# A long-convolution and Mish-MLP kernel: its visits on another calendar

## The chip, the cores and the metric

The kernel runs on one core of one Trainium2 chip. The metric is the device time of one execution in microseconds (us), lower is better; the time given for a version is the median of its runs. TensorE is called PE, its weight loads PEld; VectorE is DVE, ScalarE is ACT, GpSimd is POOL, and SyncE is SP, which here only issues DMAs.

## The reference

Two branches share one input of 2048 positions by 448 channels, and their sum is returned:

```
xn = layernorm(q)                                  # over the 448 channels
A: kv = (short causal convolution of k, 4 taps) * v
   y  = causal convolution of kv with ssm_k, 2048 taps per channel, by FFT
   A  = xn * (y + kv * ssm_D)
B: B  = mish(xn @ w1 + b1) @ w2                    # 448 -> 1792 -> 448
out  = q + A + B
```

## The kernel before

**The MLP sets the beat.** The positions are cut into 8 chunks of 256, and the 1792 hidden features into 7 pairs of 128, which makes 56 pairs in all (`pairs`). Each pair takes two half steps (`mlp_slot`). In an even half step 2i, PE does the first product of pair i (`g1_mm`, L449, 22 matmuls; every operand is split into a rounded part and a remainder, XH/XL, w1h/w1l, so that one product becomes three). In the odd half step 2i+1, ACT applies Mish (L457) and rounds (ach, L72), DVE forms the remainder (acl, L73), and PE does the second product (`g2_mm`, L474 to L476, 12 matmuls) of the pair two before. In what follows g1 and g2 are these two products.

**Once per chunk** come other steps, always at the same half steps: the layernorm statistics and POOL's normalising; four transposes each at half steps 14c+11 and 14c+12 (`ln_T`, L409), with their split into XH (ACT, L421) and XL (DVE, L419). The transposes take their PSUM tile from the same two buffers as g1, so the g1 of 14c+12 waits until the XL of 14c+11 is done. At 14c+18 the evacuation qt (`g2_evac`, L481, DVE) frees the two PSUM tiles into which the next chunk's first g2 writes, at 14c+19, and SP stores the result (L486).

**The FFT branch is fitted in between by a calendar.** The lists in the diff below give the half step of each visit; `plan` holds what is issued ahead of the half step's own work, `plan2` what comes behind it. The branch has four stages:

- f1 visits (`f1_mm`, L123), eight for h, the long filter (`H_AT`), and eight for kv (`KV_AT`). Each is followed by a fold: ACT copies one PSUM tile (L129), DVE adds and subtracts (L130, L132), and three half steps later ACT's queue stores st into Dh or Dkv (L138). st has two buffers.
- kv's taps on DVE, in four parts u0 to u3 per group, spread over the distance d between two visits of kv: u0 is one product (L152), u1 and u3 two half products and a sum (L154, L156, L161), u2 a product and a sum (L152, L161), and u3 ends with the product by v (L164). k and v are loaded by SP some half steps ahead (L143, L147).
- octets (`OCT_AT`: first half step, distance): per octet a visit to transform h (L197, one ahead), one for kv (L197), products on DVE (L230), and the first inverse transform i1 (L242) four later; its result qe goes to E in DRAM. `H0_AT` is the first of these visits.
- last steps (`I2_AT`: half step to two chunks): E is loaded (L277, SP for one chunk and POOL for seven), DVE folds e (L282, L284) three half steps ahead, PE does i2 (L300), and the gate follows (L310 to L318).

Queues run in order: what stands ahead of an instruction on its engine must have started first, and SP issues its DMAs one after the other, each when its own waits are over. The weights come as well: w1 and w2 are loaded and split over the first 16 half steps (`w1_split`, `w2_split`; w2l is the remainder, L73).

Of the kernel before, what the change touches and what calls it, by code (L numbers as in the profile page):

```python
# [22 lines left out]

G2_LAG = 2
H_HEAD = 1
H_AT = {2: 4, 3: 8, 0: 12, 4: 16, 5: 20, 6: 26, 7: 32}
KV_AT = (24, 29, 34, 39, 44, 50, 55, 60)
H0_AT = 63
OCT_AT = (65, 3)
I2_AT = {98: (6, 7), 102: (0, 1), 106: (2, 3), 111: (4, 5)}  # L30
LATE = 2
WARM = 3
WARM_N = 448
# [3 lines left out]
def tile_kernel(ctx: ExitStack, tc, q, k, v, sk, hT, sD, w1, b1, w2, c_f1, c_g, c_gi, c_i2, out):  # L37
# [51 lines left out]
    def at(slot, fn, *args):  # L89
        plan.setdefault(int(slot), []).append((fn, args))  # L90
# [182 lines left out]
    def e_load(c):  # L273

        e = EE[c] = t3([128, 2, 2, D], "e3", 4)
        src = E[:, :, :, :, c].rearrange("h j k m b d -> (j k m) h (b d)")
        (nc.sync if c == I2_AT[min(I2_AT)][1] else nc.gpsimd).dma_start(e.rearrange("p h b d -> p h (b d)"), src)  # L277

# [242 lines left out]

    for g, t in H_AT.items():
        if g != 2:
# [8 lines left out]
    for g in range(-2, 0):  # L532
        at(12, k_load, g)
    for g, t in enumerate(KV_AT):
        d = t - (KV_AT[g - 1] if g else t - 6)
        at(t - d - (3 if g > 1 else 2), k_load, g)
# [15 lines left out]
    for o in range(NO):  # L552
        s, d = OCT_AT[0] + OCT_AT[1] * o, OCT_AT[1]
        h = s - 1 if o else H0_AT
        at(h - d if o else h - 2, o_load, AH, Dh, o, "ah")
# [10 lines left out]

    ts = sorted(I2_AT)
    for n, t in enumerate(ts):
        for m, c in enumerate(I2_AT[t]):
            at(ts[n - 2] + 1 if n > 1 else ts[0] - 4 + n, e_load, c)  # L570
# [119 lines left out]
```

## Time and profile before

| | |
|---|---|
| median of 3 runs | 381.12 us (379.84 to 381.22) |
| profiled execution | 380.68 us, of it 378.9 us from first to last instruction |
| PE busy | 365.5 us (96%) |
| DVE busy | 270.0 us (71%) |
| ACT busy | 165.9 us (44%) |
| POOL busy | 52.7 us (14%) |
| mean granted PE clock | 0.994 |

PE is busy in nearly every slice, so the time is PE's work plus what it waits. A row of the waits names who waited, for whom, the sum in us, how often, and the longest. A row of the timeline has start, length, engine, line, operation, and in brackets the idle time ahead of it with what ended it. Matmuls overlap, so the distance from one start to the next tells more than a length.

### The profile page before, as it was taken

Reading aid. Unit: us, or ns where it says so; the run is one execution under the profiler, and the core shown is the slowest. Engines: PE = TensorE matmul, PEld = TensorE weight load, DVE = VectorE, ACT = ScalarE, POOL = GpSimd, SP = SyncE. Lnnn points to the kernel's source line nnn. Section 1 sums busy time; section 2 is a strip of 40 time slices with the busy share of each in tenths; the row PEclk is TensorE's granted clock in tenths of the full one; section 3 lists DMA queues with packets and bytes.
Section 4 is the critical chain, followed back from the end, with each engine's and each line's share of the span. In section 5 each row is a group of like instructions: output and inputs, shape, how many; then the busy total and the mean of one; then the engine's idle time right before and its main releaser. Section 6 shows DMA issues by size and latency. Waiting matters only on the chain.

```text
span 378.9 us, 7964 instructions
## 1 busy us (share of the span) xinstructions
PE 365.5 (96%) x3382; PEld 295.2 (78%) x3382; DVE 270.0 (71%) x357; ACT 165.9 (44%) x277; POOL 52.7 (14%) x46
## 2 busy tenths in 40 slices
PE   5999999999999999999999999999999999999994
PEld 1788888968888989889877666666666879889883
DVE  2889858999999998997525747655465733897651
ACT  2677553343341443243353555545465433225440
POOL 2106100700033001400005000060000002112101
PEclk9899999999999999999999999999999999999999
DMA  7699996829587429514775498897495477739927
GB/s 269 246 293 354 363 337 159 251 80 284 134 283 220 98 62 271 162 43 99 242 240 201 138 273 233 264 269 212 144 289 159 91 195 300 258 150 317 185 68 145
DMA packets 31988, 79.38 MB, mean 210 GB/s; under 512 B 2897, under 2 KB 18130, under 8 KB 31954
## 3 DMA queue, kind: packets, MB, share of 16 engines
q1 hardware_dynamic: 20754, 47.22, 37.4%
q10 hardware_dynamic: 9328, 22.50, 23.2%
q0 software_dynamic: 1872, 9.18, 8.7%
q8 instruction: 26, 0.43, 0.4%
q14 instruction: 8, 0.07, 0.0%
HBM read 50.44 MB, written 28.44 MB: 208 GB/s over the span
## 4 chain that ended last, share of the span: by engine, by line
PE 75%; DVE 10%; DMA 7%; ACT 3%; issue 2%; ACTq 0%; SPq 0%; DVEq 0%
PE pg L449 30%; PE pg L474 10%; PE pg L475 9%; PE pg L476 9%; PE pc L197 7%; PE pc L242 4%; DMA qt<-in_q_dram 3%; PE pc L123 3%; PE pc L300 2%; DVE x L161 2%; DMA kr<-in_k_dram 1%; DVE st L130 1%; DMA Dkv<-st 1%; PE pg L409 1%; DVE x L152 1%
## 5 line engine op out<-in xcount | busy, mean ns | idle before, releaser
L457 ACT ACTIVATE a<-pg,b1t 128x256 f32<-128x256 f32 x112 | 47.1, 473 | 108.7 <-PE pg L449 88.3
L449 PE MATMUL pg<-XH,w1h 128*128 128x256 f32 x448 | 91.3, 285 | 1.6 <-DVE XL L419 0.9
L449 PEld LDWEIGHTS pg<-XH,w1h 128*128 128x128 f32 x448 | 69.7, 188 | 18.8 <-issue 15.8
L474 PE MATMUL pg<-w2h,ach 128*128 128x448 f32 x224 | 83.4, 372 | 0.2 <-DVE qt L481 0.2
L475 PE MATMUL pg<-w2l,ach 128*128 128x448 f32 x224 | 81.4, 363 | 0.6 <-DVE w2l L73 0.6
L476 PE MATMUL pg<-w2h,acl 128*128 128x448 f32 x224 | 81.4, 363 | 0.0
L73 DVE TENSOR_TENSOR acl<-a,ach 128x512 fp32r<-128x512 f32 x56 | 38.5, 688 | 58.7 <-ACT ach L72 58.5
L449 PE MATMUL pg<-XL,w1h 128*128 128x256 f32 x448 | 69.7, 277 | 0.0
L449 PEld LDWEIGHTS pg<-XL,w1h 128*128 128x128 f32 x448 | 59.4, 188 | 0.2 <-DVE XL L419 0.2
L449 PE MATMUL pg<-XH,w1l 128*128 128x256 f32 x336 | 56.9, 278 | 0.0
L474 PEld LDWEIGHTS pg<-w2h,ach 128*128 128x128 f32 x224 | 42.0, 187 | 12.9 <-issue 9.8
L449 PEld LDWEIGHTS pg<-XH,w1l 128*128 128x128 f32 x336 | 46.9, 188 | 0.0
L390 POOL TENSOR_TENSOR rstd<-ve,mhalf 128x2 f32<-128x2 f32 (+1 forms) x9 | 8.6, 958 | 268.3 <-DVE ve L387 268.3
L475 PEld LDWEIGHTS pg<-w2l,ach 128*128 128x128 f32 x224 | 42.1, 188 | 3.4 <-DVE w2l L73 1.1
L476 PEld LDWEIGHTS pg<-w2h,acl 128*128 128x128 f32 x224 | 42.1, 188 | 2.7
L72 ACT CAST ach<-a 128x512 fp32r<-128x512 f32 x56 | 34.7, 620 | 1.8
L394 POOL TENSOR_SCALAR xn<-qt,mv,rstd 128x448 f32<-128x448 f32 x12 | 27.4, 2292 | 0.6
L161 DVE TENSOR_TENSOR x<-x 128x896 f32<-128x896 f32 x24 | 27.0, 1123 | 0.8
L421 ACT CAST XH<-pg 128x512 fp32r<-128x512 f32 x16 | 9.4, 588 | 38.9 <-PE pg L409 38.8
L419 DVE TENSOR_TENSOR XL<-pg,XH 128x512 fp32r<-128x512 f32 x16 | 11.0, 688 | 15.0 <-ACT XH L421 14.8
L129 ACT COPY st<-pc 128x896 f32<-128x896 f32 x16 | 14.6, 909 | 16.0 <-PE pc L123 13.3
L123 PE MATMUL pc<-x,f1id 32*64 32x448 f32 x256 | 17.3, 585 | 3.5 <-DMA f1id<-in_c_f_dram 3.5
(63 smaller groups left out, 395.9 us busy)
## 6 DMA issues: line engine op xcount, KB each, us to landing
Dh<-st ACTq DMA_DIRECT2D x16, 448.0 KB, 5.5
Dkv<-st ACTq DMA_DIRECT2D x16, 448.0 KB, 5.2
ah<-Dh SPq DMA_DIRECT2D x8, 896.0 KB, 7.1
av<-Dkv SPq DMA_DIRECT2D x8, 896.0 KB, 6.5
E<-qe ACTq DMA_DIRECT2D x16, 448.0 KB, 5.0
e<-E POOLq DMA_DIRECT2D x7, 896.0 KB, 8.4
kr<-in_k_dram SPq DMA_DIRECT2D x10, 448.0 KB, 7.0
x<-in_hT_dram SPq DMA_DIRECT2D x8, 448.0 KB, 6.5
```

The source lines that it names most:

```text
L72: nc.scalar.copy(h, raw)
L73: V.tensor_sub(l, raw, h)
L123: nc.tensor.matmul(ps[h][64 * jj:64 * jj + 64, b, :D], f1[rg:rg + 32, 0:64], x[rg:rg + 32, jj], start=True, stop=True, tile_position=(rg, ...
L161: V.tensor_add(KV[g], KV[g], o)
L197: nc.tensor.matmul(p[32 * t:32 * t + 32, r, :D], g[rs, t, c], a[rs, t], start=True, stop=True, tile_position=(64 * r, 32 * t))
L242: nc.tensor.matmul(ps[t // 2][cg:cg + 32, t % 2, :D], gi[ts, r, c, 32 * jj:32 * jj + 32], Y[o][c][ts, r], start=c == 0, stop=c == 1, tile_ ...
L394: eng.tensor_scalar(xn[:, jj, :D], Q[c][:, jj], mv[:, j, 0:1], rstd[:, j:j + 1], op0=ALU.subtract, op1=ALU.mult)
L449: nc.tensor.matmul(ps[:, n], l, r, start=n_ == 0, stop=n_ == len(mm) - 1)
L457: nc.scalar.activation(a[:, n], ps[:, n], AF.Mish, bias=b1t[:, 2 * p + n:2 * p + n + 1])
L474: nc.tensor.matmul(ps, ah[:, n, cs], w2h[:, f], start=f == 0, stop=False)
L475: nc.tensor.matmul(ps, ah[:, n, cs], w2l[:, f], start=False, stop=False)
L476: nc.tensor.matmul(ps, al[:, n, cs], w2h[:, f], start=False, stop=f == NF - 1)
```

## The change

Only the five lists change; the work is the same.

```diff
-H_AT = {2: 4, 3: 8, 0: 12, 4: 16, 5: 20, 6: 26, 7: 32}
-KV_AT = (24, 29, 34, 39, 44, 50, 55, 60)
-H0_AT = 63
-OCT_AT = (65, 3)
-I2_AT = {98: (6, 7), 102: (0, 1), 106: (2, 3), 111: (4, 5)}
+H_AT = {2: 4, 3: 8, 0: 11, 4: 14, 5: 16, 6: 18, 7: 21}
+KV_AT = (24, 29, 35, 40, 46, 51, 57, 62)
+H0_AT = 65
+OCT_AT = (67, 3)
+I2_AT = {99: (6, 7), 103: (0, 1), 107: (2, 3), 111: (4, 5)}
```

What hangs on a visit moves with it: folds, stores, loads, taps, products. The octets' last i1 moves from half step 90 to 92, the first i2 from 98 to 99.

DVE around half step 11, where chunk 1 is transposed. Before:

```order
L419 TENSOR_TENSOR XL<-pg_488,XH 128x4x128
L73 TENSOR_TENSOR acl<-a,ach 128x512
L73 TENSOR_TENSOR w2l<-kr,w2h 128x896
L419 TENSOR_TENSOR XL<-pg_533,XH 128x4x128
L130 TENSOR_TENSOR st<-pc,st 128x896
L132 TENSOR_TENSOR st<-pc,st 128x896
```

Changed:

```order
L419 TENSOR_TENSOR XL<-pg_500,XH 128x4x128
L73 TENSOR_TENSOR acl<-a,ach 128x512
L130 TENSOR_TENSOR st<-pc,st 128x896
L132 TENSOR_TENSOR st<-pc,st 128x896
L73 TENSOR_TENSOR w2l<-kr,w2h 128x896
L419 TENSOR_TENSOR XL<-pg_539,XH 128x4x128
```

The fold of h's visit 0 (L130, L132) moved ahead of the split of w2's fifth pair (w2l).

DVE from half step 20 on, from the u2 of kv's group 0 to its product by v. Before, the fold of half step 20 stands ahead of it:

```order
L130 TENSOR_TENSOR st<-pc,st 128x896
L387 TENSOR_SCALAR ve<-mv 128x2
L132 TENSOR_TENSOR st<-pc,st 128x896
L152 TENSOR_TENSOR x<-kr,skb 128x896
L161 TENSOR_TENSOR x<-x 128x896
L73 TENSOR_TENSOR acl<-a,ach 128x512
L154 TENSOR_TENSOR x<-kr,skb 128x448
L156 TENSOR_TENSOR x<-kr,skb 128x448
L161 TENSOR_TENSOR x<-x 128x896
L164 TENSOR_TENSOR x<-x 128x896
```

Changed, a fold (of half step 21) stands between u2 and u3; two more, of 16 and 18, are done ahead of this piece:

```order
L152 TENSOR_TENSOR x<-kr,skb 128x896
L161 TENSOR_TENSOR x<-x 128x896
L73 TENSOR_TENSOR acl<-a,ach 128x512
L130 TENSOR_TENSOR st<-pc,st 128x896
L132 TENSOR_TENSOR st<-pc,st 128x896
L154 TENSOR_TENSOR x<-kr,skb 128x448
L156 TENSOR_TENSOR x<-kr,skb 128x448
L161 TENSOR_TENSOR x<-x 128x896
L164 TENSOR_TENSOR x<-x 128x896
```

Around half step 32, where chunk 1 is evacuated (qt). DVE before and changed:

```order
L154 TENSOR_TENSOR x<-kr,skb 128x448
L156 TENSOR_TENSOR x<-kr,skb 128x448
L161 TENSOR_TENSOR x<-x 128x896
L164 TENSOR_TENSOR x<-x 128x896
L73 TENSOR_TENSOR acl<-a,ach 128x512
L481 TENSOR_TENSOR qt<-pg_746,qt 128x448
L481 TENSOR_TENSOR qt<-pg_750,qt 128x448
```

```order
L73 TENSOR_TENSOR acl<-a,ach 128x512
L154 TENSOR_TENSOR x<-kr,skb 128x448
L156 TENSOR_TENSOR x<-kr,skb 128x448
L161 TENSOR_TENSOR x<-x 128x896
L164 TENSOR_TENSOR x<-x 128x896
L481 TENSOR_TENSOR qt<-pg_785,qt 128x448
L481 TENSOR_TENSOR qt<-pg_789,qt 128x448
```

u3 of kv's group 2 and an acl changed places, and u3 now stands directly ahead of qt. SP at the same place, before and changed:

```order
L366 DMA qt<-in_q_dram 128x896
L143 DMA kr<-in_k_dram 128x896
L486 DMA out_dram<-qt 128x896
L147 DMA x<-in_v_dram 128x896
L143 DMA kr<-in_k_dram 128x896
```

```order
L366 DMA qt<-in_q_dram 128x896
L486 DMA out_dram<-qt 128x896
L143 DMA kr<-in_k_dram 128x896
L147 DMA x<-in_v_dram 128x896
L143 DMA kr<-in_k_dram 128x896
```

The load of k for group 3 (kr) moved from ahead of the store of qt to behind it.

## Prediction

> **What bounds the kernel now.** I read the page's first part, the waits of PE, the chain that ended last, and then the timeline at the places that the calendar moves.
>
> ```profile
> PE 365.5 (96%) x3382; PEld 295.2 (78%) x3382; DVE 270.0 (71%) x357; ACT 165.9 (44%) x277; POOL 52.7 (14%) x46
> PE pg L449 <- DVE XL L419: 0.9, 2, 0.5
> PE pg L475 <- DVE w2l L73: 0.6, 1, 0.6
> PE pc L197 <- ACT hs L208: 0.5, 1, 0.5
> 311.17 2.51 PE pg L449 x22
> 316.08 2.51 PE pg L449 x22
> 318.59 0.44 PE pg L409 x4
> 303.99 2.06 PE pc L242 x64
> 326.79 1.66 PE pc L300 x32
> ```
>
> The first row is the page's, the next three are waits, the rest the chain with start, length and work. PE is the bound: 365.5 of 378.9 us. The calendar neither adds nor removes an instruction, so only waits of PE can change. The chain gives PE's unit costs: a first product (g1) takes 2.51, and the next starts 4.91 after it, so a second product (g2) takes 2.40. An f1 visit takes 0.94 (first two rows below), i1 2.06, i2 1.66. A visit also costs about 0.1 on either side (2.72 instead of 2.51 for a g1 between two visits, an estimate from the chain), and a group of four transposes 0.44 with its edge.
>
> ```profile
> 65.07 1.01 PE L123 MATMUL pc<-x,f1id 32*64 32x448 f32 x16
> 66.01 0.62 PE L449 MATMUL pg<-XH,w1h 128*128 128x256 f32 x3
> ...
> 186.07 0.52 PE L449 MATMUL pg<-XH,w1h 128*128 128x256 f32 x3
> ```
>
> These starts are g1 of half steps 20 and 62. Between them lie 21 g1 and 21 g2 (103.1), ten f1 visits (9.4), six groups of transposes with edges (2.6) and the edges of the visits (2.1): 117.2. It took 120.06, so about 2.8 us was lost, more than the waits view's idle time, because some of it sits in drawn-out matmuls. That is what the middle of the change can win. DVE, the engine that PE waits for there, is full. The first ten rows are a consecutive run of it in the timeline (start, length); the others are used with it:
>
> ```profile
> 95.80 1.09 DVE L130 TENSOR_TENSOR st<-pc,st 128x896 f32<-128x896 f32 x1
> 96.92 1.09 DVE L132 TENSOR_TENSOR st<-pc,st 128x896 f32<-128x896 f32 x1
> 97.93 1.08 DVE L152 TENSOR_TENSOR x<-kr,skb 128x896 f32<-128x896 f32 x1
> 99.05 1.09 DVE L161 TENSOR_TENSOR x<-x 128x896 f32<-128x896 f32 x1
> 100.06 0.62 DVE L154 TENSOR_TENSOR x<-kr,skb 128x448 f32<-128x448 f32 x1
> 100.59 0.62 DVE L156 TENSOR_TENSOR x<-kr,skb 128x448 f32<-128x448 f32 x1
> 101.24 1.09 DVE L161 TENSOR_TENSOR x<-x 128x896 f32<-128x896 f32 x1
> 102.37 1.09 DVE L164 TENSOR_TENSOR x<-x 128x896 f32<-128x896 f32 x1
> 103.38 0.68 DVE L73 TENSOR_TENSOR acl<-a,ach 128x512 fp32r<-128x512 f32 x1
> 103.98 1.15 DVE L481 TENSOR_TENSOR qt<-pg,qt 128x448 f32<-128x448 f32 x2
> 104.65 0.47 PE L474 MATMUL pg<-w2h,ach 128*128 128x448 f32 x1
> 67.12 1.09 DVE L130 TENSOR_TENSOR st<-pc,st 128x896 f32<-128x896 f32 x1 [1.10 <-ACT st L129]
> 136.36 2.73 PE pg L449 x22
> 140.64 0.69 DVE acl L73
> ```
>
> From start to next start: acl 0.60, a fold (L130, L132) 2.13, tap u2 2.13, tap u3 with the product by v 3.32 (so u1, without that product, about 2.2, and u0 1.0), XL like acl 0.60. The new chunk's g2 starts 0.67 after the evacuation qt starts (103.98 to 104.65). A fold starts 2.05 after its f1 (65.07 to 67.12), an acl 4.3 after its g1 (136.36 to 140.64).
>
> **The change, part by part.**
>
> *Half step 11, +0.6.* h's visit 0 now stands beside the transposes, and DVE does its fold ahead of w2l. Counted from the start of that f1, the transposes end at 1.4. ACT then runs XH (0.7 with its start, an estimate from XL's 0.6), Mish and ach (1.7, which is 4.3 less a g1 of 2.6) and the fold's copy (0.7 of the 2.05 that lie between an f1's start and its fold), to 4.5. The fold takes 2.13 and w2l about 1.0, like a fold's half, to 7.6. PE wants w2l at 7.1: transposes to 1.45, g2 2.4, transposes 0.45, g1 2.6, and one matmul 0.2. So 0.5 to 0.6 is lost. The waits view has such a wait of 0.6 for w2l, at another visit beside a w2 split. Bounds: 0, and 1.1 for one w2l.
>
> *Half steps 14 to 26, +2.0.* h's visits 4 to 7 now put folds at 16, 18 and 21. The fold of 16 costs nothing: DVE still had idle time (1.10 ahead of the fold at 67.12, half step 20). If that cover were gone, up to 1.1 would be added to what follows. From the fold of 18 to the XL of 25, which g1 of 26 waits for, DVE has no idle: three folds 6.4, u1 twice 4.4, u2 twice 4.3, u3 3.3, u0 1.0, three acl and XL 2.4, the statistics of a chunk 1.4, and 0.6 because taps run slower beside POOL's normalising (an estimate; u0 took 1.49 instead of 1.08 in a row below): 23.8. With 2.05 ahead and 0.1 behind, XL is there 25.9 after the f1 of 18. PE wants it after four g1 and four g2 (19.6), three f1 with edges (3.4) and two groups of transposes (0.9): 23.9 to 24.1. The wait is 1.8, and 0.2 more falls on the f1 of 24, whose product ends about when PE arrives. Bounds 0.8 (the old loss there) and 4, if ACT's copy at 18 also waits for the store issued at 17 (stores of this kind land in 4.1 to 10.8 us, median 5.4, by this row; at the median the wait is about nothing).
>
> ```profile
> DMA to landing us min/median/max: 4.1/5.4/10.8
> ```
>
> *The loads of h, nothing.* On SP they pass w2's, skb's and k's loads, each by one or two loads of 448 KB. k's first load then comes about 2 us later; its use, u0 of 17, comes 1.2 later too, since PE has done one more f1. That leaves the fold and the taps of 17 and 18 as cover; if it is gone, up to 2 us are added at 26.
>
> *Half step 32, +1.4.* kv's group 2 moves by one, and its u3 comes from after 30 to after 31, directly ahead of qt. From the start of g1 of 30: acl 4.3, itself 0.6, u3 3.32, then 0.67 to the matmul: 8.9. PE arrives after g1, g2, g1 = 7.4. So 1.4 to 1.5, whatever DVE's lag. Before, the late qt cost 0.2 here.
>
> *Half steps 32 to 40, +0.8.* On SP, k's load for group 3 now stands behind the store of qt instead of ahead of it. The row of before with the same order:
>
> ```profile
> 144.55 0.34 SPq L486 DMA_DIRECT2D out_dram<-qt  x1
> 144.95 0.93 SPq L143 DMA_DIRECT2D kr<-in_k_dram  x1
> 150.59 1.49 DVE L152 TENSOR_TENSOR x<-kr,skb 128x896 f32<-128x896 f32 x1 [1.07 <-DMA kr<-in_k_dram]
> DMA to landing us min/median/max: 4.5/7.0/9.1
> ```
>
> The store waits for qt, and u0 starts 6.04 after it. From the end of qt: 6.1, then u0 to XL of 39 (u0 twice 2.0, u1 2.2, two acl and XL 1.8, fold 2.1, u2 2.1, u3 3.3, statistics 0.8), to 20.5. PE reaches g1 of 40 19.8 after qt. Wait 0.8; with a load that lands in 4.5 nothing, in 9.1 about 4. I take the row with this very order, 5.6.
>
> *Half steps 41 to 61, +0.4.* The waits of 46 and 54, part of the 2.8, go: at 45 no tap stands ahead of qt, and at 53 DVE is 1 us ahead. At 60, qt follows u3 of 58: from f1 of 57, 2.05, fold 2.13, u2 2.13, u3 3.32, acl 0.6 and 0.67 make 10.9; PE needs 10.5.
>
> These make 4.6 (0.2, 1.8, 1.4, 0.8, 0.4) where 2.8 was lost: +1.8. With half step 11: +2.4.
>
> *Octets, -0.35.* Two waits of 0.5 arose where octet visits met transposes at 67 and 81 (the row of hs is one). Now only 81 and 82 meet: -0.5. Two groups of transposes lose a neighbour to share edges with: +0.15. From the last f1 of kv to av's first use there are five half steps as before, so whatever PE waits for av stays. POOL's order is the same, and on SP only qt's loads and stores change places with loads that have three half steps (some 9 us with a visit in each) until their use: nothing.
>
> *Octets to last steps, +2.2.* The last i1 moves by two, the first i2 by one.
>
> ```profile
> 307.72 1.25 ACTq L254 DMA_DIRECT2D E<-qe  x2
> 313.79 0.38 SPq L277 DMA_DIRECT2D e<-E  x1
> 314.56 2.54 POOL L277 DMA_DIRECT2D e<-E  x3 [2.39 <-ACT a L457]
> 322.93 1.09 DVE L282 TENSOR_TENSOR ex<-e 128x896 f32<-128x896 f32 x1 [1.16 <-DMA e<-E]
> 326.19 1.09 DVE L284 TENSOR_TENSOR e<-e 128x896 f32<-128x896 f32 x1
> 318.00:320.00 2.00, 2.00 (x16) 1.94 (x15) 0.32 (x1) 0.93 (x3) 0.00 (x0) 1.00 1.04 427
> ```
>
> i1 ended at 306.05; the store of E, its landing, the load of e and four DVE operations (two folds of e) end at 327.28, 21.2 later. i2 started at 326.79, 20.7 after i1, and its second half, 0.8 later, needs the last of them: 0.3 of slack. In the new calendar PE arrives after 92 to 98: four g1, three g2, two groups of transposes and edges, 18.3 after i1. The second half may start at 21.3 instead of 19.1: 2.2 us. The load is the part that could change: it took 8.4 while four loads of 896 KB and two of q ran, DMA at 427 GB/s (last row). The same six are still issued together. Bounds: 1.2, if store and load each gain 0.5, and 3.
>
> By the Trainium skill (DMA: Bandwidth & Descriptors, section Anatomy of one DMA) a single transfer takes about 2.0 us plus its bytes over 436 GB/s; for 917,504 bytes that gives an estimate of 4.1 us, and by it i2 would not wait and the sum would be 2.2 lower. The row's 8.4 contradicts it for loads that share the engines.
>
> **Sum.** 2.4 - 0.35 + 2.2 = +4.25. The profiled execution took 380.68 (378.9 of span and 1.8 around it); 384.9. The median of the runs, 381.12, is 0.4 higher, inside their spread of 379.84 to 381.22, so I say 385.0.
>
> **Rivals.** *Relief (faster).* Two folds (4.3) leave the stretch in which DVE is full, and the stretch gains two half steps (4.9). If DVE therefore never keeps PE waiting, the 2.8 and the 0.5 go, the tail's wait is eaten by quicker loads, and 377.5 results. For it: DVE's idle time past half step 41. Against: the waits at 26 and 32 come from what stands directly ahead, not from the total. It decides if XL of 25 is ready within 24 us of the f1 of 18 and e's fold within 19.
>
> *Nothing to tell.* Half of the new DVE waits (2.3 instead of 4.6) and 1.2 at the tail: 381.6. Less than 0.5% (1.9 us) cannot be told from no change here.
>
> *The clock falls.* If a wait grows past 3 us, PE slows:
>
> ```profile
> PE pc L123 <- DMA f1id<-in_c_f_dram: 3.5, 1, 3.5
> 9.00:10.00 1.00, 0.96 (x16) 0.36 (x16) 0.75 (x3) 0.00 (x0) 0.99 (x2) 0.50 0.99 329
> 13.00:14.00 1.00, 0.78 (x6) 0.78 (x7) 0.94 (x3) 1.00 (x3) 0.00 (x0) 1.00 0.23 90
> ```
>
> After the idle 3.5 us at the start the granted clock was 0.50 from 9 to 12, then 1.00. A wait of 3.5 at i2 (1.3 above mine) and some 3.4 us at half speed (1.7): 388. The Trainium skill (TensorE: Matmul & The Clock Gate, section Why this matters for your kernels) says likewise that an idle gap of over about 3 us halves the clock. No row here shows waits between 1 and 3 us.
>
> **Chances.** Waits as summed 0.62, the clock or a very late k load 0.10, nothing to tell 0.20, relief 0.08. Slower 0.72, same 0.20, faster 0.08. The main case alone spans 383 to 387; 381.0 to 388.5 takes in the second and third.
>
> **What would show it.** In the changed profile: PE waiting for XL before g1 of 26 (1.8), for qt at 33 (idle plus a late start, 1.4), for w2l at 13; DVE idle 4 to 5 us for kr at 33; PE waiting for e's fold at i2 of 99 (2.2); waits of hs or qe halved. I am wrong if DVE is not late at 25 and 32, or if i2 of 99 starts on time; then the time falls by those terms.

## The result and the profile after

| | before | changed |
|---|---|---|
| median of the runs | 380.71 us (379.84 to 381.22, 4 runs) | 386.93 us (386.69 to 387.45, 4 runs) |
| ratio to before, 95% interval | | 1.0162 [1.0139, 1.0185] |
| profiled execution, its span | 380.68, 378.9 | 386.76, 385.0 |
| mean granted PE clock | 0.994 | 0.987 |

The changed calendar is slower by 1.6%: 6.2 us by the medians, 6.1 by the two spans, where the parts of the forecast add up to 4.25.

The first part of the page, then the waits of PE in the changed kernel (engine, tile, line, who was waited for: sum in us, times, longest):

```profile
PE 368.0 (96%) x3382; PEld 297.5 (77%) x3382; DVE 269.7 (70%) x357; ACT 165.7 (43%) x277; POOL 53.2 (14%) x46
PE pc L123 <- DMA f1id<-in_c_f_dram: 2.5, 1, 2.5
PE pg L474 <- DVE qt L481: 1.6, 2, 1.3
PE pg L449 <- DVE XL L419: 1.5, 1, 1.5
PE pc L242 <- DVE yc L230: 0.8, 1, 0.8
PE pc L123 <- DVE x L164: 0.6, 1, 0.6
PE pg L475 <- DVE w2l L73: 0.6, 1, 0.6
PE pc L197 <- ACT hs L208: 0.5, 1, 0.5
```

PE is 2.5 us busier (368.0 after 365.5) with the same 3382 matmuls: where it waits between two matmuls of one group, part of the loss is written down as longer matmuls. So the places are better measured by starts. The order of g1 and g2 is the same in all versions, and at the half steps in the table below each version has done the same visits. The distance is taken from the g1 of half step 10, where the start, which varies from run to run (see the last section), is over, to the last g2. They stand in the timeline like this, before and changed:

```profile
37.19 0.51 PE L449 MATMUL pg<-XH,w1h 128*128 128x256 f32 x3
370.88 0.36 PE L474 MATMUL pg<-w2h,ach 128*128 128x448 f32 x1
```

```profile
36.46 0.51 PE L449 MATMUL pg<-XH,w1h 128*128 128x256 f32 x3
376.54 0.36 PE L474 MATMUL pg<-w2h,ach 128*128 128x448 f32 x1
```

From the one to the other it took 333.69 us before and 340.08 after, 6.39 more. Ahead of half step 10 the changed kernel was 0.73 early by luck (see the last section), and behind the last g2 it took 0.44 longer; together 6.1. The same distance, worked out from the starts in the timelines of all the versions below (us since the g1 of half step 10; read the rows with the experiments):

| version | g1 of 36 | g1 of 62 | g1 of 92 | g1 of 100 | last g2 |
|---|---|---|---|---|---|
| before | 76.46 | 148.88 | 273.82 | 296.22 | 333.69 |
| changed | 79.83 | 151.89 | 277.10 | 302.41 | 340.08 |
| h_back | 76.21 | 148.16 | 273.27 | 298.30 | 335.97 |
| h67_back | 76.17 | 148.12 | 273.13 | 298.25 | 335.94 |
| h_only | 78.88 | 151.42 | 276.48 | 298.88 | 336.35 |
| kv2_back | 79.57 | 151.51 | 276.55 | 301.57 | 339.34 |
| norm_pool | 79.69 | 151.74 | 275.96 | 300.89 | 338.67 |
| e_later | 80.28 | 152.33 | 277.57 | 302.53 | 340.21 |
| i2_later | 80.47 | 152.52 | 277.49 | 300.06 | 338.73 |
| e_queue | 79.54 | 151.59 | 276.67 | 299.18 | 336.96 |
| e_pool | 80.39 | 152.44 | 277.48 | 300.00 | 337.78 |
| mend_11 | 76.17 | 148.13 | 272.33 | 294.94 | 332.72 |
| mend_12 | 75.90 | 147.85 | 272.12 | 294.73 | 332.51 |

By stage the change cost 3.37 up to half step 36, gave back 0.36 from there to 62 (the waits that kv's old calendar had), cost 0.27 in the octets, 2.91 around the first i2 and 0.20 behind it.

Four places of the changed timeline (start, length, engine, line, operation; in brackets the idle time ahead and what ended it). First the stretch of h and kv:

```profile
46.78 0.48 PE L475 MATMUL pg<-w2l,ach 128*128 128x448 f32 x1 [0.57 <-DVE w2l L73]
63.36 0.91 ACT L129 COPY st<-pc 128x896 f32<-128x896 f32 x1 [2.85 <-DMA Dh<-st]
64.30 1.09 DVE L130 TENSOR_TENSOR st<-pc,st 128x896 f32<-128x896 f32 x1 [1.00 <-ACT st L129]
86.92 0.68 DVE L419 TENSOR_TENSOR XL<-pg,XH 128x512 fp32r<-128x512 f32 x1
87.65 0.62 PE L449 MATMUL pg<-XH,w1h 128*128 128x256 f32 x3 [1.54 <-DVE XL L419]
105.97 1.09 DVE L164 TENSOR_TENSOR x<-x 128x896 f32<-128x896 f32 x1
106.98 1.15 DVE L481 TENSOR_TENSOR qt<-pg,qt 128x448 f32<-128x448 f32 x2
107.74 0.44 PE L474 MATMUL pg<-w2h,ach 128*128 128x448 f32 x1 [1.33 <-DVE qt L481]
```

PE waits for w2l at 13, for XL ahead of the g1 of 26, and for qt at 33, whose tap u3 (L164) stands right ahead of it. The fold of 18 (64.30) itself began a microsecond late, because ACT's copy waited for a store of h out of the two buffers of st. Next, group 3 of kv behind that qt:

```profile
108.15 0.34 SPq L486 DMA_DIRECT2D out_dram<-qt  x1
108.55 0.42 SPq L143 DMA_DIRECT2D kr<-in_k_dram  x1
112.60 1.09 DVE L152 TENSOR_TENSOR x<-kr,skb 128x896 f32<-128x896 f32 x1 [3.35 <-DMA kr<-in_k_dram]
```

The load of k is behind the store of qt, as predicted, but u0 starts 4.45 after the issue of the store, where the row of before with this order had 6.04. XL of 39 was in time and PE did not wait at 40. Then the last octet's product and the last i1:

```profile
308.65 1.08 DVE L230 TENSOR_TENSOR yd<-vs,hs 128x896 f32<-128x896 f32 x1
308.82 1.48 POOL L390 TENSOR_TENSOR rstd<-ve,mhalf 128x2 f32<-128x2 f32 x1 [61.43 <-DVE ve L387]
310.34 0.94 DVE L394 TENSOR_SCALAR xn<-qt,mv,rstd 128x448 f32<-128x448 f32 x2 [0.61 <-POOL rstd L390]
311.31 0.23 DVE L398 COPY xn<-xn 128x128 f32<-128x128 f32 x1
311.45 1.08 DVE L230 TENSOR_TENSOR yc<-yc,yd 128x896 f32<-128x896 f32 x1
312.59 1.05 PE L242 MATMUL pc<-yc,gi 32*32 32x448 f32 x32 [0.80 <-DVE yc L230]
```

DVE normalises the last chunk (L394, L398) in the middle of the product: it waits 0.61 for POOL's rstd (L390), and only then does the last operation of the product, for which the second half of i1 waits. Last, the chain from E to the first i2:

```profile
315.42 1.25 ACTq L254 DMA_DIRECT2D E<-qe  x2
321.50 0.38 SPq L277 DMA_DIRECT2D e<-E  x1
322.26 2.47 POOL L277 DMA_DIRECT2D e<-E  x3 [11.96 <-PE pg L409]
331.05 1.09 DVE L282 TENSOR_TENSOR ex<-e 128x896 f32<-128x896 f32 x1 [5.16 <-DMA e<-E]
335.45 0.57 PE L300 MATMUL pc<-e,i 64*32 64x448 f32 x2 [0.18 <-DVE e L284]
```

The i1 ended at 313.56, its store was issued at 315.42, the loads from 321.50 on; the first fold started 9.55 after that (8.79 after the issue of its own load, the first of POOL's three), and the second half of i2 could begin at 335.45, 21.9 after i1. i2 took 4.15 from its start to the next g2, against 1.66 in the step at 103.

### The profile page after: what moved, and what is told of

Same layout as the page of the kernel before. It is cut to its first block, busy times and chain, and to the rows that moved or that the text cites. A ratio compares the mean times of both kernels' runs of the same rounds, so it can differ in the third digit from the quotient of the medians.

```text
span 385.0 us, 7965 instructions
## 1 busy us (share of the span) xinstructions
PE 368.0 (96%) x3382; PEld 297.5 (77%) x3382; DVE 269.7 (70%) x357; ACT 165.7 (43%) x277; POOL 53.2 (14%) x46
## 4 chain that ended last, share of the span: by engine, by line
PE 68%; DVE 13%; DMA 8%; issue 4%; ACT 4%; POOL 1%; ACTq 0%; POOLq 0%; DVEq 0%; SPq 0%
PE pg L449 27%; PE pg L474 9%; PE pg L475 8%; PE pg L476 8%; PE pc L197 7%; PE pc L242 3%; PE pc L123 3%; DMA e<-E 2%; DVE x L161 2%; DVE st L130 2%; PE pc L300 2%; PE pg L409 2%; DMA E<-qe 1%; DMA Dh<-st 1%; DVE st L132 1%
## 5 line engine op out<-in xcount | busy, mean ns | idle before, releaser
L449 PEld LDWEIGHTS pg<-XH,w1h 128*128 128x128 f32 x448 | 70.8, 190 | 16.5 <-issue 12.2
L449 PEld LDWEIGHTS pg<-XL,w1h 128*128 128x128 f32 x448 | 60.3, 190 | 0.0
L390 POOL TENSOR_TENSOR rstd<-ve,mhalf 128x2 f32<-128x2 f32 (+1 forms) x9 | 9.2, 1025 | 265.9 <-DVE ve L387 265.9
L394 POOL TENSOR_SCALAR xn<-qt,mv,rstd 128x448 f32<-128x448 f32 x12 | 27.1, 2264 | 0.6
L130 DVE TENSOR_TENSOR st<-pc,st 128x896 f32<-128x896 f32 x16 | 17.4, 1088 | 7.1 <-ACT st L129 6.7
```

What stands on the lines that cost most here:

```text
L130: V.tensor_add(st[:, 0], e, st[:, 1])
L394: eng.tensor_scalar(xn[:, jj, :D], Q[c][:, jj], mv[:, j, 0:1], rstd[:, j:j + 1], op0=ALU.subtract, op1=ALU.mult)
L449: nc.tensor.matmul(ps[:, n], l, r, start=n_ == 0, stop=n_ == len(mm) - 1)
```

## Experiments

Theory A is that of the prediction: each wait is made by what stands directly ahead of it on DVE, and the tail by a chain of fixed length. Ratios are to the kernel before, run on the same chip (381.07, 380.98 and 381.24 us in the three groups), with 95% intervals.

### h's old half steps in the changed calendar (h_back)

```diff
-H_AT = {2: 4, 3: 8, 0: 11, 4: 14, 5: 16, 6: 18, 7: 21}
+H_AT = {2: 4, 3: 8, 0: 12, 4: 16, 5: 20, 6: 26, 7: 32}
```

> The changed calendar with h's old half steps (12, 16, 20, 26, 32); kv, octets and last steps stay new. Theory A (each wait is made by what stands directly ahead of it on DVE): the new losses at half steps 13 (0.9 us) and 24 (0.6) go, the one at 26 shrinks from 1.5 to the old 0.8, and the wait for qt at 33 (1.3) shrinks by about 1, because PE does one more f1 at 32 before it arrives. 386.9 - 3.2 = 383.7 us. Theory B (DVE has too much to do in the whole stretch of h and kv; a wait taken away at one place comes back at the next): the waits move to 40 and 46 and the time stays within 1 us of 386.9.

Measured: 383.06 us, 1.0051 [1.0029, 1.0074]. The waits of PE for XL (at 26) and for qt (at 61; none is left at 33):

```profile
PE pg L449 <- DVE XL L419: 0.5, 1, 0.5
PE pg L474 <- DVE qt L481: 0.2, 1, 0.2
```

Up to half step 36 it is 3.6 us quicker than the changed kernel, and nothing comes back at 40 or 46. Theory B falls. At half step 62 this version is even 0.72 ahead of before, so the spread of kv's groups does gain, as the prediction's step on 46 and 54 had it.

### Only h's visits 6 and 7 back (h67_back)

```diff
-H_AT = {2: 4, 3: 8, 0: 11, 4: 14, 5: 16, 6: 18, 7: 21}
+H_AT = {2: 4, 3: 8, 0: 11, 4: 14, 5: 16, 6: 26, 7: 32}
```

> The changed calendar with only h's visits 6 and 7 back (26 and 32); visits 0, 4 and 5 stay at 11, 14 and 16. Theory A (the folds of 18 and 21 make the waits at 24 and 26, and the f1 of 32 covers the wait for qt at 33; the fold of 11 makes the wait for w2l and stays): 384.0 us, 0.9 more than with all of h's visits back (383.06). Rival (the folds of 14 and 16 fill DVE): the wait at 26 stays at 1.5, 386 us.

Measured: 383.29 us, 1.0063 [1.0044, 1.0083].

```profile
PE pg L475 <- DVE w2l L73: 0.6, 1, 0.6
PE pg L474 <- DVE qt L481: 0.2, 1, 0.2
```

No wait for XL is left, and none for the product of 24; the 0.2 for qt is at 61. The wait for w2l at 13 stays, and yet the stretch is as short as with all of h's visits back (76.17 and 76.21 at half step 36). With h's old half steps PE waits 0.5 for XL at 26; here the fold of 20 is done at 16, that wait is gone, and the 0.85 lost at 13 are made good (which fold made the 0.5 was not tested by itself). So visits 0, 4 and 5 cost nothing net, and all of h's cost is the folds of 18 and 21 and the f1 that is missing at 32. Theory A is right on the places, and 0.9 off where it adds them up.

### Only h's new half steps, in the kernel before (h_only)

```diff
-H_AT = {2: 4, 3: 8, 0: 12, 4: 16, 5: 20, 6: 26, 7: 32}
+H_AT = {2: 4, 3: 8, 0: 11, 4: 14, 5: 16, 6: 18, 7: 21}
```

> The kernel before with only h's half steps changed (11, 14, 16, 18, 21); kv, octets and last steps stay old. Theory A (most of the loss is h's): losses of 0.85 at half step 13, 0.7 at 24, 0.9 more at 26, and about 0.8 at 33, since PE reaches it without the f1 of 32; 381.1 + 3.3 = 384.4 us. Rival (folds taken out of kv's stretch relieve DVE there, so that h's move pays by itself and only kv and the tail cost): 381 us or less.

Measured: 383.45 us, 1.0070 [1.0049, 1.0091].

```profile
PE pg L449 <- DVE XL L419: 2.0, 2, 1.6
PE pc L123 <- DVE x L164: 0.8, 1, 0.8
PE pg L474 <- DVE qt L481: 0.4, 2, 0.2
```

h alone costs 2.66 us from half step 10 to the end, 2.42 of it by 36; the rival falls. The wait for qt at 33 is 0.25 and not 0.8: with u3 after half step 30, as before, the missing f1 of 32 does little. The wait of 1.3 in the changed kernel needs both, u3 one half step later and PE there one visit sooner.

### kv's group 2 back at 34 (kv2_back)

```diff
-KV_AT = (24, 29, 35, 40, 46, 51, 57, 62)
+KV_AT = (24, 29, 34, 40, 46, 51, 57, 62)
```

> The changed calendar with kv's group 2 back at half step 34 (all else new), so that u3 stands after half step 30 again and the k load of group 3 ahead of the store of qt. Theory A: the loss at half step 33 falls from 1.4 us to the 0.2 of before; 385.7 us. Theory B: the same u3 delays XL or qt elsewhere; 386.9 us.

Measured: 386.32 us, 1.0137 [1.0113, 1.0160]. The waits for qt, at 33 and 61, are now 0.6 together, and from the g1 of 24 to that of 36 it takes 0.92 us less than in the changed kernel. The intervals of the two ratios overlap, so the time alone does not tell. Part of the gain is hidden in it: the f1 of 24 waited 1.3 in this run and 0.6 in the changed one (it varied from 0.3 to 1.3 over the versions with these h visits, with the landing of h's stores: in this run ACT's copy at 21 waited 1.66 for one, in the changed kernel not at all). Theory A holds, with 0.9 for 1.2.

### POOL normalises the last chunk (norm_pool)

```diff
-        eng = nc.gpsimd if 0 < c < NCHUNK - 1 else V
+        eng = nc.gpsimd if c else V
```

> The changed calendar with the last chunk normalised by POOL, as the chunks before it are, instead of DVE. Theory A: the last octet's product is late at half step 92 because DVE normalises in the middle of it (0.6 us idle for rstd, 0.94 for the two normalisations and 0.2 for the copy); without them the product is ready about 1.8 us sooner, the wait of 0.8 at the last i1 goes and the wait at the first i2 stays: 386.2 us. Rival (the product is late because it began late, its input from ACT): the wait stays, 386.9 us. Second rival: POOL's normalising slows DVE and the wait at i1 keeps half its size, 386.5 us.

Measured: 386.75 us, 1.0153 [1.0127, 1.0178]. That alone cannot be told from the changed kernel's 1.0162, but the trace tells. The last operation of the product, and the second half of i1:

```profile
309.68 1.09 DVE L230 TENSOR_TENSOR yc<-yc,yd 128x896 f32<-128x896 f32 x1
311.45 0.98 PE L242 MATMUL pc<-yc,gi 32*32 32x448 f32 x17
```

yc ends at 310.77 and i1 (from 310.67) waits no more. From 62 to 92 this version takes 0.99 less than the changed one. Theory A holds, both rivals fall.

### Four loads of E on one queue (e_later, e_queue, e_pool)

To see whether the loads share the engines, the loads for chunks 0 and 1 were first put two half steps later:

```diff
-            at(ts[n - 2] + 1 if n > 1 else ts[0] - 4 + n, e_load, c)
+            at(ts[n - 2] + 1 if n > 1 else ts[0] - 4 + 3 * n, e_load, c)
```

> The changed calendar with the loads of E for chunks 0 and 1 issued two half steps later (97 instead of 95), so that only the loads for chunks 6 and 7 and two of q run at first. Theory A (the loads that run together share the DMA engines): the load that ex of half step 96 waits for takes 5 to 6 us instead of 9.1, and the 2.7 us lost at the first i2 fall to nothing; 384.2 us. Rival (the length of such a load is its own, by its descriptors): it still takes 9, and 386.9 us. Second rival: the two late loads are not there at 103, a new wait of some us, 388 or more.

Measured: 387.74 us, 1.0181 [1.0156, 1.0206]. It tells nothing, because it delayed nothing:

```profile
324.50 2.47 POOL L277 DMA_DIRECT2D e<-E  x3 [11.98 <-PE pg L409]
```

POOL still issues three loads in a row, with no wait between them. The row puts POOL's idle time ahead of them down to PE; SP's load, which waits for the store of E, was issued 0.8 earlier, so the same store is the likelier cause. The 0.8 us by which the median is above the changed kernel's is not a cost of this edit: this run reached half step 10 at 38.22 instead of 36.46, and from there to the last g2 the two agree within 0.2. Next, the four loads went on SP's queue in the order of their use:

```diff
-        (nc.sync if c == I2_AT[min(I2_AT)][1] else nc.gpsimd).dma_start(...)
+        (nc.sync if c in (6, 7, 0, 1) else nc.gpsimd).dma_start(...)
```

> The changed calendar with the loads of E for chunks 6, 7, 0 and 1 all on SP's queue, in this order, instead of one on SP and three on POOL. (To issue the loads of chunks 0 and 1 two half steps later did not delay them: all of them wait for the same store of E, and POOL issued all three at once.) Theory A (loads on several queues share the engines, those on one queue are served one after the other): the first fold's load takes 4 to 6 us instead of 9, the 2.7 us at the first i2 go; 384.3 us. Rival (a load of this shape takes 9 us by itself, or one queue serves its loads at once too): 386.9 us, within 0.7.

Measured: 384.90 us, 1.0100 [1.0080, 1.0121].

```profile
315.82 1.25 ACTq L254 DMA_DIRECT2D E<-qe  x2
321.89 0.92 SPq L277 DMA_DIRECT2D e<-E  x2
326.63 1.09 DVE L282 TENSOR_TENSOR ex<-e 128x896 f32<-128x896 f32 x1 [0.34 <-DMA e<-E]
```

From the issue of its load to the fold it is now 4.74 us instead of 8.79 (9.55 from the first load issued), i2 takes 1.67, and the stage from 92 to 100 is 2.80 shorter. The Trainium skill (DMA: Bandwidth & Descriptors, section Anatomy of one DMA) gives an estimate of 4.1 us for a transfer of this size alone, by a fit for loads that GpSimd issues; the row of the load that is served first, issued by SP, agrees with it within 0.7, while for the load that shared with the others the prediction was right not to go by it. Last, all of them on POOL's queue:

```diff
-        (nc.sync if c == I2_AT[min(I2_AT)][1] else nc.gpsimd).dma_start(...)
+        nc.gpsimd.dma_start(...)
```

> The changed calendar with all loads of E on POOL's queue (chunk 7 too, which was on SP's). With the first four on SP's queue the first fold's load took 4.7 us instead of 9.5. Theory A1 (loads of one queue are served one after the other, whatever the queue): the same here, 5 to 6 us, and 384.5 us. Theory A2 (it is POOL's queue that serves its loads side by side): 9 to 10 us again, and 387 us.

Measured: 385.12 us, 1.0107 [1.0083, 1.0131].

```profile
301.91 2.56 SPq L291 DMA_DIRECT2D q<-in_q_dram  x3
323.36 0.97 POOL L277 DMA_DIRECT2D e<-E  x1 [11.96 <-PE pg L409]
328.82 1.09 DVE L282 TENSOR_TENSOR ex<-e 128x896 f32<-128x896 f32 x1 [1.82 <-DMA e<-E]
```

5.46 us, and the same 2.8 gained. This run has one more difference: with no load of E ahead of them on SP, the loads of q left some 20 us earlier (301.91) and no longer share. But in e_queue all six loads stand on SP's queue, and here four of 896 KB on POOL's still let the first land early. So it is not the kind of queue: with the loads of E on one queue the first is served first, on SP's as on POOL's. In the changed kernel the load of chunk 6, the first on POOL's queue, ran beside chunk 7's and two of q on SP's, and the folds began late.

### The first i2 one half step later (i2_later)

```diff
-I2_AT = {99: (6, 7), 103: (0, 1), 107: (2, 3), 111: (4, 5)}
+I2_AT = {100: (6, 7), 103: (0, 1), 107: (2, 3), 111: (4, 5)}
```

> The changed calendar with the first last step (i2 of chunks 6 and 7) one half step later, at 100 instead of 99. Theory A (the chain from the last i1 over the store and load of E to the folds has a fixed length, so PE loses what it arrives early): PE arrives 2.4 us later, the 2.7 lost at the first i2 fall to 0.3; 384.5 us. Rival (the last steps themselves run too close: pushed together, 100 and 103, they wait for DVE's folds and gates instead): the loss turns up at 103; 386.9 us.

Measured: 385.54 us, 1.0119 [1.0094, 1.0144]. Both are right in part. From 92 to 100 it takes 2.74 less. But the step at 103 now waits for its own folds, which stand behind those of chunks 6 and 7 and their gates on DVE:

```profile
345.14 1.09 DVE L284 TENSOR_TENSOR e<-e 128x896 f32<-128x896 f32 x1
346.28 0.11 PEld L300 LDWEIGHTS pc<-e,i 64*32 64x32 f32 x2 [0.56 <-DVE e L284]
```

i2 of 103 takes 2.68 instead of 1.66, and 1.0 of the gain is gone.

### The mends together (mend_11, mend_12)

```diff
-H_AT = {2: 4, 3: 8, 0: 11, 4: 14, 5: 16, 6: 18, 7: 21}
+H_AT = {2: 4, 3: 8, 0: 11, 4: 14, 5: 16, 6: 26, 7: 32}
-        (nc.sync if c == I2_AT[min(I2_AT)][1] else nc.gpsimd).dma_start(...)
+        (nc.sync if c in (6, 7, 0, 1) else nc.gpsimd).dma_start(...)
-        eng = nc.gpsimd if 0 < c < NCHUNK - 1 else V
+        eng = nc.gpsimd if c else V
```

> The changed calendar with three mends together: h's visits 6 and 7 back (26, 32), the last chunk normalised by POOL, and the first four loads of E on SP's queue. If the losses add: from the g1 of half step 10 to the last g2 it took 335.9 with visits 6 and 7 back alone; POOL's normalising gives back 0.8 (the wait at the last i1), the queue 2.8 (the first i2); 332.3, where before took 333.7. The time is then 1.4 below before: 379.6 us, a ratio of 0.996. Rival (PE, now earlier, waits somewhere new, for the gates and folds of the later last steps or for the loads of chunks 2 and 3): 381 us, no better than before.

Measured: 379.78 us, 0.9957 [0.9942, 0.9972], faster than both kernels, and than before by 0.4%. Its waits for w2l, hs and qt (of the two for w2l, one is at 13 and one, 0.56, still ahead of half step 10; qt's is at 61):

```profile
PE pg L475 <- DVE w2l L73: 1.1, 2, 0.6
PE pc L197 <- ACT hs L208: 0.5, 1, 0.5
PE pg L474 <- DVE qt L481: 0.2, 1, 0.2
```

From half step 10 to the last g2 it takes 332.72, 0.97 less than before and 7.36 less than the changed kernel. The parts are 4.14 (h67_back), 1.41 (norm_pool) and 3.12 (e_queue), 8.67 in all. They overlap by 1.3: h67_back and norm_pool hold 0.6 of the wait at i2 between them (the stage from 92 to 100), and norm_pool and e_queue 0.4 of the varying wait at 24 (up to 36); 0.3 more lies from 62 to 92. In the second, w2l of 11 stands ahead of the fold again:

```diff
-H_AT = {2: 4, 3: 8, 0: 11, 4: 14, 5: 16, 6: 26, 7: 32}
+H_AT = {2: 4, 3: 8, 0: 12, 4: 14, 5: 17, 6: 26, 7: 32}
```

> The same three mends with h's visit 0 at 12 instead of 11 and visit 5 at 17 instead of 16, so that w2l of half step 11 stands ahead of the fold again. Theory A: the wait for w2l at 13 (0.6 idle, 0.85 with what is drawn out) goes and nothing else changes: 378.8 us, ratio 0.994. Rival (the fold of 17 comes into the stretch of u0 to u3 of kv's group 0 and PE waits for XL at 26, as it does for 0.5 with all of h's old half steps): 379.6 us.

Measured: 380.08 us, 0.9965 [0.9948, 0.9981], no different from mend_11. The wait for w2l at 13 is gone, but only 0.27 of the 0.85 is left at half step 36 and 0.2 at the end. No wait for XL came in its place. The rest came back between the g1 of 18 and that of 22, in products drawn out by 0.1 to 0.3 each (the g1 of 18 took 2.79, not 2.50); by what stays open.

## Why the prediction came out as it did

385.0 was forecast, slower, with 381.0 to 388.5; it became 386.9. Point by point, in us:

| step | forecast | measured, and where |
|---|---|---|
| w2l at 11/13 | +0.6 | 0.57 idle, 0.85 with what is drawn out (g2 of 13 took 3.35, not 2.41 to 2.50) |
| f1 of 24 | +0.2 | 0.6 |
| XL ahead of g1 of 26 | +1.8 | 1.54 idle, 1.7 with the transposes drawn out |
| qt at 33 | +1.4 | 1.33 idle, 1.4 |
| k load, g1 of 40 | +0.8 | nothing |
| qt at 61 | +0.4 | 0.25 idle, 0.4 |
| old losses that go | -2.8 | -1.9, an estimate |
| all up to 62 | +2.4 | +3.0 |
| octets | -0.35 | +0.3 |
| last steps | +2.2 | +2.9, and 0.2 behind |

**Right:** the mechanism, and most of the places. Counting DVE's work from an f1 or a g1 forward to the XL or qt that PE needs gave the waits at 26, 33 and 61 within 0.3, and w2l's idle time. The chain from i1 to i2 was also right link by link. That the waits came from what stands directly ahead, and not from the total of DVE's work, is shown by h_back, h67_back and kv2_back, where they went one by one.

**The k load at 40** failed at its duration. The order on SP was as read; u0 could start 4.05 after the load's issue, where I took the one row of the same order, 5.6. My own lower bound, "with a load that lands in 4.5 nothing", was what happened. One row of a load is one draw from a wide range (4.5 to 9.1 in the view of before); the kernel had slack for a quick one.

**The credit of 2.8** was too large, and that it is not seen in the sum is luck. Counted with the prediction's own unit costs, the changed kernel's way from the g1 of 20 to that of 62 holds 116.1 us of work (nine f1 visits instead of ten) and took 121.08, so 5.0 are lost there. The waits named above explain 4.1 of them (0.6, 1.7, 1.4, 0.4). So about 0.9 of the 2.8 did not go; in the sum this stands against the 0.8 of the k load, which did not come. Where the 0.9 sit stays open.

**The f1 of 24** was mis-sized (0.2, measured 0.6, and 0.3 to 1.3 over the runs): the store of h does hold back ACT's copy, 2.85 at the fold of 18, which I had put into the upper bound only.

**The octets** failed at a step that I costed at nothing. I had compared the queues of SP and POOL and the meetings with transposes; the 0.5 of one such meeting went as said. But the last octet moved by two half steps onto the normalising of the last chunk, which alone of all the later chunks is done by DVE. Before, the product ended long ahead of it:

```profile
303.75 1.07 DVE L230 TENSOR_TENSOR yc<-yc,yd 128x896 f32<-128x896 f32 x1
315.85 1.09 DVE L394 TENSOR_SCALAR xn<-qt,mv,rstd 128x448 f32<-128x448 f32 x2
```

Now the wait for rstd and the normalising stand inside the product, and i1 waits 0.8. norm_pool shows it.

**The tail** was mis-sized: 2.2, measured 2.9. The load took 0.4 longer (9.55 instead of 9.14 from the first load issued, 8.79 instead of the prediction's 8.4 from its own issue), the store was issued 0.1 later, and 0.3 fell on the g1 of 98, drawn out. That the load is long because it shares was only argued; e_queue and e_pool show it.

**Where to look for the cause** was the weakest part. I charged qt at 33 to kv's group 2. The wait needs h's visit 7 to have left 32 as well: with either undone, 0.3 to 0.4 is left of the 1.4 (the g1 of 32 and what is lost behind it take 2.89 to 3.02, not 4.01). And w2l's 0.6 is real at its place and free in sum, since a PE that is held up at 13 comes later to 26. Waits of one stretch do not add.

The rivals: nothing to tell falls by the ratio, 1.0162 [1.0139, 1.0185]. Relief is refuted by h_only, since folds taken out of kv's stretch slow it down; but the part of it about kv is true (0.72 gained by 62 in h_back). The clock did not fall behind half step 10: in the page's slices it is 9 tenths or more there in all but the very last, and no single wait of PE there was longer than 1.54.

## What to carry to other kernels

When work is moved off a crowded stretch of an engine, count the work between the last fixed start and the next result that the bound engine needs, at every place that it lands on, and look also for a rare operation there (a first or last iteration done by another engine). Put loads that are wanted at different times on one queue in the order of their use: here the first was then usable in about half the time, and the later steps took only 0.1 us longer. And compare traces from a common point behind the start; a sum of single waits is an upper bound, since a wait early in a stretch pays for a later one.

## What the runs showed of the hardware that I had not expected

**Queues.** Four loads of 896 KB and two of 448 KB kept the DMA engines full either way: 400 to 435 GB/s from 324 to 334 us in the changed kernel, 394 to 416 in e_queue. Split over two queues, the load that is wanted first was usable 8.79 us after its issue; with all six on SP's queue, after 4.74; with the four on POOL's and those of q gone before, after 5.46.

**The start is a lottery.** Up to half step 10 the changed kernel and kv2_back have the same calendar, and the one reached its g1 at 36.46 us, the other at 38.36. PE's wait for the first load, f1id, lay between 2.1 and 4.7, and in 10 of the 13 traces the granted clock was 0.50 for a while around it. Two stretches of the timeline at 14 us (length, then busy time of PE, PEld, DVE, ACT and POOL, granted clock, DMA share, GB/s), of the changed kernel and of h_back, and h_back's wait:

```profile
14.00:16.00 2.00, 2.00 (x11) 2.00 (x11) 1.94 (x3) 0.48 (x1) 0.00 (x0) 0.50 0.39 111
14.00:16.00 2.00, 2.00 (x20) 2.00 (x19) 1.91 (x4) 1.09 (x3) 0.00 (x0) 1.00 0.36 59
PE pc L123 <- DMA f1id<-in_c_f_dram: 3.1, 1, 3.1
```

After a wait of 2.5 the changed kernel was still at 0.50 there; after one of 3.1 h_back was back at 1.00. The Trainium skill (TensorE: Matmul & The Clock Gate, section Why this matters for your kernels) puts the fall at idle gaps of over about 3 us; here it also came after 2.5, and the length of the wait did not tell how long the slow clock lasted. In the three other traces (h_only, i2_later, e_pool; waits of 2.1 to 2.9) the clock is recorded as 1.00 throughout, yet the first g1 took 4.41 to 4.76 us, as in the changed kernel at 0.50 (4.45) and not as in h_back (2.93); so there the record may have missed the fall. No wait behind half step 10 (up to 1.5) lowered the clock. This start is likely one reason why runs of one kernel spread over 2 to 3 us (380.17 to 382.91 for before in one group; only one run of each version was traced), and it is why the differences above are taken from half step 10 on.
